# A fused attention, mixture-of-experts and gated-convolution kernel: routing steps, copies and weight splits moved, and one product done in halves of 64 columns

## The chip, the cores and the metric

One Trainium2 chip, one core of it. The metric is the device time of one launch in microseconds (us).

## The reference

Float32 throughout; B=2 batches, S=768 tokens, 8 heads of 64, so rows of D=512. Three stages follow each other.

```python
# 1. decaying linear attention, per batch and head
state = gamma * state + outer(k[t], v[t]);  y[t] = q[t] @ state / 8
# 2. mixture of 8 experts, one per token, with a sticky choice
logits = x @ w_gate;  local_gate = sigmoid(x @ w_local)
e = argmax(logits[s]) if s == 0 or local_gate[s] < 0.5 else prev_e
out[s] = softmax(logits[s])[e] * (relu(x[s] @ w1[e]) @ w2[e])    # 512 -> 1024 -> 512
# 3. gated convolution over tokens
h = relu(x @ w_in);  c = conv1d(h, conv_w, 3 taps)
out = (h * sigmoid(c)) @ w_out                                   # 512 -> 1024 -> 512
```

The weights of stage 3 arrive as float64 and are decoded on the chip.

## The kernel before

**Attention** runs over 12 tiles of 128 tokens (6 per batch), and each tile's steps are written out by hand. For tile i TensorE does Z (q times the state so far, `a_Z`), X of tile i-1 (`a_X`), AV (`a_AV`: masked scores A times v), U (`a_U`: the state's update) and S of tile i+1 (`a_S`: q times k). X multiplies a tile's transposed output xT by xw, a matrix of identity blocks with the gate's columns beside them: it turns the tile so that tokens are on partitions and gives the routing logits (128 columns and 9) at once. ScalarE copies xT, the state Z, the tile xo that goes to the scratch tensor scr in DRAM, builds the decay tables (`a_table`) and scales half of v; GpSimd scales the other half of v (`a_scale_v`) and q of the tile after the next (`a_scale_q`); VectorE masks the scores (L352) and does the routing. The constants are one array in DRAM: the table tq is loaded in two halves (L1106), the rest as one tile C (L1107) that also holds the factors gv (for v) and gq (for the tables). Ten small products at the start (`keep_warm`) keep TensorE busy until q is there.

**Routing** (`route`) handles the tiles in groups of 3, 3, 3, 2 and 1. It is a generator: `part(g)` runs one more step of group g (the largest logit and a code; a scan that finds the last fresh choice; the one-hot matrix; counts; slots). `logits(i)` copies a tile's logits out of PSUM (L440, L441).

**Experts.** Each weight unit (128 x 1024) is loaded into one of 4 raw buffers (`load_unit`, on SP's queue), cast by ScalarE to its high part whi (`split_first`, L172) and subtracted by VectorE to its low part wlo (`split_second`, L181); then its raw buffer is free for the next load. Every product of the experts is three: high x high, high x low, low x high. Expert 0 starts before routing has ended, as half an expert (`alone(0, 0)`) on 128 rows gathered early (x0); `back` turns a layer's result with four transposes, after which VectorE makes its low part hl (L644). Then comes a branch for overflowing experts (`overflow`, not taken here), then the other half (`alone(0, 1)`, fed by `T(0, (1,))`, which makes xsh and xsl, L585), then experts 1 to 6 whole (`L1`, `L2`), and expert 7 in two halves. Between these, `dec_first` and `dec_second` decode stage 3's weights: two operations of ScalarE, five of VectorE (L218 to L224) and two last ones (L226, L227) on GpSimd or, where `last=nc.vector` says so, on VectorE. Near the end of expert 7 the rows of stage 3 are gathered (`c_gather`), scaled by VectorE (`c_scale`, L938) and transposed (`c_T`, L946).

All engines run their instructions in the order in which this code issues them, which is the order of the work; a read of a PSUM bank by ScalarE waits for an earlier read of that bank by VectorE.

Of the kernel before, what the change touches and what calls it, by code (L numbers as in the profile page):

```python
# [97 lines left out]
def tile_kernel(ctx: ExitStack, tc: tile.TileContext, consts, qk, kv, w1, w2, w_in, conv_w, w_out, out):  # L98
# [28 lines left out]
    n0 = off["gv"][0]  # L127
# [3 lines left out]
    def cv(name):  # L131
        a, b = off[name]
        return C[:, a - n0:b - n0]
# [132 lines left out]
    tabs = [ld.tile([P, NP * P], F32, name="tq", tag="tq", bufs=1)]  # L266
# [52 lines left out]
    def a_scale_q(i, engine, a=slice(0, 2)):  # L319
# [5 lines left out]
        engine.tensor_tensor(out=t, in0=t, in1=tabs[i % NC].rearrange("p (a n) -> p a n", a=2)[:, a], op=ALU.mult)  # L325

    def a_scale_v(i):
        if i >= NT:
# [10 lines left out]
    def a_S(i, ms=(0, 1)):  # L339

        t = qk_t[i]
        for m in ms:
# [5 lines left out]
        if ms[-1] == 0:  # L348
            return
# [50 lines left out]
    def a_X(i):  # L400
# [3 lines left out]
        for p in range(NP):  # L404
            o = (p % 2) * P
            nc.tensor.matmul(x_t[i][p // 2][:, o:o + XN], lhsT=xT[:, p, :], rhs=xw[:, p, :],
                             start=(p % 2 == 0), stop=(p % 2 == 1), skip_group_check=True)

    def a_store(i):
# [9 lines left out]
        nc.scalar.dma_start(out=scr[1 + i * P:1 + (i + 1) * P, :], in_=xo)  # L419
# [23 lines left out]
    def route(g):  # L443
# [55 lines left out]
        else:  # L499
            ve.tensor_copy(c_, end)  # L500
        at_ = tmp([P, n, E], "at")
# [101 lines left out]
    def moe(mo):  # L603
        xg_t, xs_t, h_t = {}, {}, {}
# [24 lines left out]
        def alone(e, half, free):  # L629
# [5 lines left out]
            def back(f):  # L635
# [8 lines left out]
                nc.vector.tensor_tensor(out=hl[:, 4 * f:4 * f + 4, sl], in0=p3, in1=dst.bitcast(F32), op=ALU.subtract)  # L644
# [112 lines left out]
        next(first)  # L757
        part(g3)
        next(first)
        next(first)  # L760
        part(g4)
        part(g3)
        next(first)
        part(g4)
        part(g3)
        next(first)
        part(g4)
        split_second(nc.vector)
        next(first)
# [3 lines left out]
        gather(0, (1,))  # L773
        for _ in route_blocks():
# [45 lines left out]
        for n, _ in enumerate(alone(e, 1, True)):  # L820
            if 8 <= n < 12:
                c_scale(n - 8)
# [422 lines left out]
```

## Time and profile before

| what | value |
|---|---|
| time, three runs | 404.12, 404.28, 405.5 us; median 404.28 |
| the profiled execution | 404.91 us; its span 403.1 us |
| TensorE matmul (PE) busy | 390.5 us, 97% |
| VectorE (DVE) busy | 294.4 us, 73% |
| ScalarE (ACT) busy | 246.7 us, 61% |
| GpSimd (POOL) busy | 113.2 us, 28% |
| moved by DMA | 73.24 MB, 182 GB/s over the span |

The span is one execution as the profiler sees it, and the time of that execution holds a little besides. An engine's busy time is what it spends in instructions; records of matmuls overlap, so a wait shorter than a record's tail does not show as idle. The waits view lists idle time and the instruction that ended it. Attention lies at 0 to 62 us, expert 0 at 62 to 94, experts 1 to 6 to 233, expert 7 to 261, stage 3 to the end.

### The profile page before, as it was taken

What the parts mean: (1) busy time and instruction counts of PE and PEld (TensorE: products, weight loads), DVE (VectorE), ACT (ScalarE), POOL (GpSimd) and SP (SyncE); (2) the same over time, 40 slices, a digit from 0 to 9 for tenths busy, and PEclk for the clock granted to TensorE, in tenths of its full rate; (3) what the DMA queues carried; (4) which work ended last, traced back from release to release, by engine and by line L of the source; (5) the groups of instructions that cost most, each with busy time, mean ns of one, the idle gap of its engine ahead of it and who ended that gap; (6) DMA issues with size and microseconds to landing.
All of it is one profiled execution on the core that took longest, in us unless ns stands there. A gap on an engine that the chain in (4) does not pass through costs nothing.

```text
span 403.1 us, 7359 instructions
## 1 busy us (share of the span) xinstructions
PE 390.5 (97%) x2772; PEld 337.5 (84%) x2772; DVE 294.4 (73%) x548; ACT 246.7 (61%) x483; POOL 113.2 (28%) x106
## 2 busy tenths in 40 slices
PE   7999998889999999999999999899999999999996
PEld 3888885568989797988989777699979789998986
DVE  3369867976799999799998858769954626990350
ACT  4886653656867675676757563578845437971531
POOL 3555510365035244363634242441000000000000
PEclk9999999999999999999999999999999999999999
DMA  8999992688879888787978131532010010001002
GB/s 295 377 355 411 323 364 107 209 266 297 302 225 327 283 314 259 244 309 263 320 265 303 60 102 47 137 112 72 0 53 27 0 54 27 2 0 52 28 0 78
DMA packets 28087, 73.24 MB, mean 182 GB/s; under 512 B 3009, under 2 KB 3649, under 8 KB 28050
## 3 DMA queue, kind: packets, MB, share of 16 engines
q1 hardware_dynamic: 19506, 54.67, 38.8%
q10 hardware_dynamic: 6240, 10.55, 7.2%
q0 software_dynamic: 2304, 7.54, 6.1%
q8 instruction: 22, 0.36, 0.4%
q14 instruction: 15, 0.12, 0.1%
HBM read 62.26 MB, written 10.49 MB: 180 GB/s over the span
## 4 chain that ended last, share of the span: by engine, by line
PE 55%; DVE 11%; issue 5%; DMA 5%; ACT 2%; POOL 2%; DVEq 0%; ACTq 0%; POOLq 0%
PE c L1041 15%; PE b L989 12%; PE c L742 11%; PE rt L989 5%; DVE wlo L181 5%; PE b L710 4%; DMA raw<-in_moe_w_dram 3%; PE state L710 2%; PE rt L710 2%; DVE hl L717 1%; DMA yg<-scr,posi 1%; ACT whi L172 1%; PE b L652 1%; PE a L946 1%; DVE xsl L585 1%
## 5 line engine op out<-in xcount | busy, mean ns | idle before, releaser
L181 DVE TENSOR_TENSOR wlo<-raw,whi 128x1024 fp32r<-128x1024 f32 x64 | 87.4, 1388 | 11.8 <-ACT whi L172 11.3
L172 ACT CAST whi<-raw 128x1024 fp32r<-128x1024 f32 x64 | 66.8, 1056 | 40.9 <-PE c L742 20.4
L1008 DVE SCALAR_TENSOR_TENSOR cs<-hs,cw,cs 128x384 f32<-128x384 f32 x64 | 39.6, 619 | 30.1 <-ACT cs L1006 29.0
L226 POOL TENSOR_TENSOR dmf<-dmf,ds 128x512 f32<-128x512 f32 x12 | 24.9, 2075 | 83.7 <-DVE ds L224 52.4
L742 PE MATMUL c<-whi,hh 128*112 128x512 f32 x96 | 38.0, 395 | 0.0
L742 PE MATMUL c<-wlo,hh 128*112 128x512 f32 x96 | 37.5, 391 | 0.0
L989 PE MATMUL b<-x,whi 128*128 128x386 f32 x176 | 37.1, 340 | 0.2 <-ACT x L956 0.2
L1041 PE MATMUL c<-whi,gh 128*128 128x512 f32 x88 | 35.2, 399 | 0.0
L1041 PE MATMUL c<-whi,gl 128*128 128x512 f32 x88 | 34.9, 396 | 0.0
L1041 PE MATMUL c<-wlo,gh 128*128 128x512 f32 x88 | 34.7, 395 | 0.0
L989 PEld LDWEIGHTS b<-x,whi 128*128 128x128 f32 x176 | 31.2, 189 | 0.8 <-ACT x L956 0.6
L742 PE MATMUL c<-whi,hl 128*112 128x512 f32 x96 | 30.0, 394 | 0.5 <-DVE hl L717 0.5
L611 POOL DMA_INDIRECT xg<-scr,permi x15 | 20.0, 1336 | 26.6 <-DVE nbi L541 19.6
L710 PE MATMUL b<-xsl,whi 128*128 128x240 f32 x96 | 26.6, 277 | 0.4 <-DVE xsl L585 0.4
L710 PE MATMUL b<-xsh,whi 128*128 128x240 f32 x96 | 26.5, 276 | 0.0
L710 PE MATMUL b<-xsh,wlo 128*128 128x240 f32 x96 | 26.3, 274 | 0.0
L352 DVE TENSOR_TENSOR A<-b,mask 128x512 f32<-128x512 f32 x24 | 15.4, 685 | 11.3 <-PE b L346 11.3
L1012 ACT ACTIVATE sg<-cs 128x384 f32<-128x384 f32 x32 | 16.6, 519 | 9.4 <-DVE gl L1018 9.1
L742 PEld LDWEIGHTS c<-whi,hl 128*112 128x112 f32 x96 | 17.1, 181 | 6.3 <-DVE hl L717 2.2
L742 PEld LDWEIGHTS c<-whi,hh 128*112 128x112 f32 x96 | 17.4, 181 | 4.3
L227 POOL TENSOR_TENSOR wdec<-dmf 128x512 f32<-128x512 f32 x12 | 20.7, 1721 | 0.9
L742 PEld LDWEIGHTS c<-wlo,hh 128*112 128x112 f32 x96 | 17.4, 181 | 4.2
(254 smaller groups left out, 1013.2 us busy)
## 6 DMA issues: line engine op xcount, KB each, us to landing
raw<-in_moe_w_dram SPq DMA_DIRECT2D x64, 512.0 KB, 4.9
qk<-in_qk_dram SPq DMA_DIRECT2D x11, 512.0 KB, 6.2
kv<-in_kv_dram SPq DMA_DIRECT2D x11, 512.0 KB, 5.9
draw<-in_moe_w_in_dram SPq DMA_DIRECT2D x8, 512.0 KB, 5.3
draw<-in_moe_w_out_dram SPq DMA_DIRECT2D x8, 512.0 KB, 4.8
scr<-xo ACTq DMA_DIRECT2D x11, 256.0 KB, 6.3
out_dram<-os ACTq DMA_DIRECT2D x11, 256.0 KB, 2.0
scr<-ys ACTq DMA_DIRECT2D x10, 256.0 KB, 3.6
```

The lines of the kernel that those rows point to most:

```text
L172: nc.scalar.copy(hi, raw[u])
L181: engine.tensor_tensor(out=lo, in0=t, in1=hi.bitcast(F32), op=ALU.subtract)
L226: last.tensor_tensor(out=f, in0=f, in1=s.bitcast(F32), op=ALU.mult)
L227: last.tensor_tensor(out=out, in0=f, in1=a.bitcast(F32), op=ALU.add)
L352: nc.vector.tensor_tensor(out=A_t[i][j], in0=sc2[j].rearrange("p (a t) -> p a t", a=NP), in1=mask.unsqueeze(1).to_broadcast([P, NP, P]), o ...
L611: nc.gpsimd.indirect_dma_start(out=t, out_offset=None, in_=xrow, in_offset=bass.IndirectOffsetOnAxis(ap=permi[:, col:col + 1], axis=0))
L710: nc.tensor.matmul(o, lhsT=a[:, fs], rhs=b_[:, dt, OFF:], start=(dt == 0 and n == 0 and ft % 2 == 0), stop=(dt == KD - 1 and n == 2), skip ...
L742: nc.tensor.matmul(yp[t][0:P - o], lhsT=a[:, ft, t * P + o:(t + 1) * P], rhs=b_[:, ws], start=(ft == 0 and a is hh and b_ is wh), stop=(ft ...
L989: nc.tensor.matmul(pb[:, 0:WN], lhsT=split[u_in + dt][wi][:, fs], rhs=x_[dt // 2][:, dt % 2, :], start=(n == 0), stop=(n == 3 * KD - 1))
L1008: nc.vector.scalar_tensor_tensor(out=cs, in0=tap[j], scalar=cw[:, j, ft:ft + 1], in1=cs, op0=ALU.mult, op1=ALU.add)
L1012: nc.scalar.activation(out=sg, in_=cs, func=AF.Sigmoid)
L1041: nc.tensor.matmul(ops[t][:, 0:n_], lhsT=a[:, ts_], rhs=b_[:, ws], start=(ft == 0 and n == 0), stop=(ft == KF - 1 and n == 2))
```

## The change

Six edits, all in the order or the form of work; what is computed stays the same.

1. gv and gq move from C into the second half of tq's load. All of tile 0's v is scaled by GpSimd, in two instructions. `a_S0` does tile 0's scores in two PSUM bank pairs and masks them in halves. Nine warming products instead of ten.
2. X is done as eight products with 64 columns of xT each, the halves in turn on the two partition halves of the same bank.
3. In tile 10 one more weight unit is cast and split; in the last tile the split before `a_U` is done before `a_X`, and routing of the last group but one starts after `a_AV`. The store of tile 10 follows the copy of x_last.
4. Two weight loads go ahead of the two loads for the decode; routing steps between the first products of expert 0 are dealt out anew, with one more pause (`yield`) for small groups, and the first `hl` waits for two of them.
5. Splits, decodes and T around the branch: splits at steps 0 and 4, T before `dec_second`, the first decode wholly on VectorE; in the second half of expert 0 the decode starts three steps later.
6. `c_scale` one step earlier in expert 7.

```diff
-    n0 = off["gv"][0]
+    n0 = off["rev"][0]
...
-        return C[:, a - n0:b - n0]
+        return tabs[0][:, a:b] if b <= n0 else C[:, a - n0:b - n0]
...
-        nc.gpsimd.tensor_tensor(out=t[:, H // 2:], in0=t[:, H // 2:],
-                                in1=g[:, H // 2:].unsqueeze(2).to_broadcast([P, H // 2, D]), op=ALU.mult)
-        for h in range(H // 2):
+        for a in ((slice(0, H // 2), slice(H // 2, H)) if i == 0 else (slice(H // 2, H),)):
+            nc.gpsimd.tensor_tensor(out=t[:, a], in0=t[:, a], in1=g[:, a].unsqueeze(2).to_broadcast([P, H // 2, D]),
+                                    op=ALU.mult)
+        for h in range(H // 2 if i else 0):
...
+    def a_S0():
+
+        t = qk_t[0]
+        A_t[0] = [at.tile([P, NP, P], F32, name=f"A{j}", tag=f"A{j}", bufs=1) for j in range(2)]
+        for m in range(2):
+            a_scale_q(0, nc.vector, slice(m, m + 1))
+            for half in range(2):
+                for j in range(2):
+                    nc.tensor.matmul((sc2, x2)[m][j][:, half * P:(half + 1) * P], lhsT=t[HALF[j], m, 1, half, :],
+                                     rhs=t[HALF[j], m, 0, half, :], start=True, stop=True)
+        for m in range(2):
+            for j in range(2):
+                nc.vector.tensor_tensor(out=A_t[0][j][:, 2 * m:2 * m + 2],
+                                        in0=(sc2, x2)[m][j][:, 0:2 * P].rearrange("p (a t) -> p a t", a=2),
+                                        in1=mask.unsqueeze(1).to_broadcast([P, 2, P]), op=ALU.mult)
...
-            nc.tensor.matmul(x_t[i][p // 2][:, o:o + XN], lhsT=xT[:, p, :], rhs=xw[:, p, :],
-                             start=(p % 2 == 0), stop=(p % 2 == 1), skip_group_check=True)
+            for half in HALF:
+                nc.tensor.matmul(x_t[i][p // 2][half, o:o + XN], lhsT=xT[:, p, half], rhs=xw[:, p, :],
+                                 start=(p % 2 == 0), stop=(p % 2 == 1), skip_group_check=True)
...
+        if n < 3:
+            yield
...
+                if (e, half, f) == (0, 0, 0):
+                    low_first.append(low)
+                else:
+                    low()
...
-            if n in (0, 1, 2, 7):
+            if n in (0, 4):
                 split_unit(nc.vector)
             if n == 3:
                 overflow(mo)
                 gather(1)
-                dec_first()
-            elif n == 4:
-                dec_second()
+                dec_first(last=nc.vector)
             elif n == 5:
                 T(0, (1,))
+                dec_second()
         for n, _ in enumerate(alone(0, 1, True)):
             if n == 0:
-                dec_first()
-            elif n == 1:
+                split_unit(nc.vector)
+            elif n == 3:
+                dec_first(mo)
+            elif n == 5:
                 dec_second()
...
-            if 8 <= n < 12:
-                c_scale(n - 8)
+            if 7 <= n < 11:
+                c_scale(n - 7)
...
-        for half in range(2):
-            a_scale_q(0, nc.vector, slice(half, half + 1))
-            a_S(0, (half,))
+        a_S0()
...
             part(due)
+            if last_tile:
+                split_second(nc.vector, False)
             if i:
                 a_X(i - 1)
                 logits(i - 1)
-                a_store(i - 1)
-            if fresh is not None:
+                store = a_store(i - 1)
+                if not last_tile:
+                    store()
+            if i == NT - 2:
+                split_first()
+            if fresh is not None and not last_tile:
                 rts[fresh] = route(fresh)
                 part(fresh)
             a_AV(i)
+            if last_tile:
+                store()
+                rts[fresh] = route(fresh)
+                part(fresh)
...
+        load_unit()
+        load_unit()
         dec_load()
         dec_load()
-        load_unit()
```

VectorE in the last two tiles, before. A is the masked scores of tile 11, LG the logits of tile 10, x_last a copy that X of tile 11 reads, R and sl routing's counts and slots.

```order
L352 TENSOR_TENSOR A_987<-b_77,mask 128x512
L352 TENSOR_TENSOR A_988<-b_78,mask 128x512
L500 CAST cnt<-rt 128x8
...
L506 TENSOR_SCALAR sl<-slot_112,R_116 128x256 x3
L440 COPY LG<-c_79 128x9
L441 TENSOR_TENSOR LG<-c_80,LG 128x9
L458 TENSOR_REDUCE MX<-LG 128x2
...
L381 COPY x_last<-a_76 128x2x128
L181 TENSOR_TENSOR wlo<-raw,whi 128x1024
```

And now:

```order
L181 TENSOR_TENSOR wlo<-raw,whi 128x1024
L367 TENSOR_TENSOR A_1029<-b_77,mask 128x512
L367 TENSOR_TENSOR A_1030<-b_78,mask 128x512
...
L524 TENSOR_SCALAR sl<-slot_112,R_116 128x256 x3
L181 TENSOR_TENSOR wlo<-raw,whi 128x1024
L456 COPY LG<-c_79 128x9
L457 TENSOR_TENSOR LG<-c_80,LG 128x9
L396 COPY x_last<-a_76 128x2x128
L474 TENSOR_REDUCE MX<-LG 128x2
```

One split moved ahead of the logits' copy and one more was added ahead of the masks; the copy of x_last moved ahead of routing's step.

VectorE after the branch, in expert 0, before (ds and dmag belong to the decode, xsl is what the second half of expert 0 waits for, ys the first half's result):

```order
L218 TENSOR_SCALAR dmag<-dmag 128x512
L219 TENSOR_SCALAR dmag<-dmag 128x512
L221 TENSOR_SCALAR ds<-draw 128x512
L222 SCALAR_TENSOR_TENSOR dmag<-dmag,ds 128x512
L224 TENSOR_SCALAR ds<-dmag 128x512
L585 TENSOR_TENSOR xsl<-a_76,xsh 128x4x128
L181 TENSOR_TENSOR wlo<-raw,whi 128x1024
L687 COPY ys<-c_79 128x512
```

And now:

```order
L181 TENSOR_TENSOR wlo<-raw,whi 128x1024
L603 TENSOR_TENSOR xsl<-a_76,xsh 128x4x128
L218 TENSOR_SCALAR dmag<-dmag 128x512
...
L224 TENSOR_SCALAR ds<-dmag 128x512
L226 TENSOR_TENSOR df<-df,ds 128x512
L227 TENSOR_TENSOR wdec_86<-df,dmag 128x512
L713 COPY ys<-c_79 128x512
L181 TENSOR_TENSOR wlo<-raw,whi 128x1024
```

xsl moved ahead of the decode, behind one split, and the decode's last two operations came over from GpSimd.

SP's queue at the end of attention, before (raw are the weight units, draw the decode's loads) and now:

```order
L163 DMA raw<-in_moe_w_dram 128x2x512 x4
L244 DMA draw<-in_moe_w_in_dram 128x1024 x2
L161 DMA raw<-in_moe_w_dram 128x1024 x4
```

```order
L163 DMA raw<-in_moe_w_dram 128x2x512 x4
L161 DMA raw<-in_moe_w_dram 128x1024 x2
L244 DMA draw<-in_moe_w_in_dram 128x1024 x2
L161 DMA raw<-in_moe_w_dram 128x1024 x2
```

Two weight loads, the units 8 and 9, moved ahead of the two loads of the decode.

## Rows read from the trace of the kernel before

**Rows 1.** The windows view: share of time busy per engine, granted clock, DMA share, GB/s.

```profile
0.00:10.00 10.00, 7.35 (x59) 3.76 (x59) 3.69 (x9) 4.48 (x13) 3.73 (x17) 1.00 0.80 293
...
10.00:20.00 10.00, 10.00 (x171) 8.89 (x175) 3.42 (x9) 8.50 (x31) 5.14 (x9) 1.00 1.01 377
...
80.00:100.00 20.00, 17.86 (x104) 14.86 (x105) 15.18 (x18) 10.72 (x15) 12.83 (x9) 1.00 0.83 278
```

**Rows 2.** Timeline, first 10 us: start, length, engine, line, out<-in, count, wait before.

```profile
5.18 0.42 DVE L325 TENSOR_TENSOR qk<-qk,tq 128x256 f32<-128x256 f32 x1 [0.51 <-DMA tq<-in_consts_dram]
...
5.83 1.16 PE L346 MATMUL b<-qk 64*128 64x128 f32 x16
...
7.04 0.61 POOL L332 TENSOR_TENSOR kv<-kv,C 128x256 f32<-128x256 f32 x1 [5.06 <-DMA C<-in_consts_dram]
...
7.81 1.43 PE L374 MATMUL a<-A,kv 128*64 128x128 f32 x16 [0.82 <-ACT kv L335]
...
9.25 0.69 DVE L325 TENSOR_TENSOR qk<-qk,wdec 128x512 f32<-128x512 f32 x1 [0.94 <-ACT wdec L316]
...
9.99 1.16 PE L346 MATMUL b<-qk 64*128 64x128 f32 x16 [0.29 <-DVE qk L325]
```

**Rows 3.** Timeline of attention tile 2: TensorE, and what ScalarE and GpSimd do beside it.

```profile
15.89 1.06 ACT L335 ACTIVATE kv<-kv,C 128x64 f32<-128x64 f32 x4
...
16.00 1.21 PE L406 MATMUL c<-xw,xT 128*128 128x137 f32 x8
...
16.08 1.27 POOL L325 TENSOR_TENSOR qk<-qk,wdec 128x512 f32<-128x512 f32 x1 [1.13 <-DMA qk<-in_qk_dram]
...
17.14 1.09 PE L374 MATMUL a<-A,kv 128*64 128x128 f32 x16
...
18.06 0.63 PE L396 MATMUL state<-kv 128*64 128x64 f32 x16
```

**Rows 4.** Timeline, end of attention and expert 0's first half: VectorE, ScalarE, TensorE.

```profile
56.96 1.04 ACT L172 CAST whi<-raw 128x1024 fp32r<-128x1024 f32 x1
...
59.09 0.16 DVE L440 COPY LG<-c 128x9 f32<-128x9 f32 x1
...
60.41 0.37 ACT L383 COPY x_last<-a 128x256 f32<-128x256 f32 x1 [0.45 <-ACT xo L416]
...
61.12 1.22 DVE L181 TENSOR_TENSOR wlo<-raw,whi 128x1024 fp32r<-128x1024 f32 x1
...
71.48 0.39 PE L671 MATMUL c<-whi,hh 128*128 128x512 f32 x1
```

**Rows 5.** The waits view of TensorE, 62 to 160 us: total, times, longest.

```profile
PE a L640 <- ACT hr L663: 1.0, 1, 1.0
...
PE b L652 <- DVE xsl L585: 1.0, 1, 1.0
...
PE rt L484 <- DVE far L470: 0.6, 1, 0.6
```

**Rows 6.** Timeline around expert 0's second half and the entry of expert 1.

```profile
79.92 0.68 DVE L585 TENSOR_TENSOR xsl<-a,xsh 128x512 fp32r<-128x512 f32 x1
...
80.52 2.25 DVE L181 TENSOR_TENSOR wlo<-raw,whi 128x1024 fp32r<-128x1024 f32 x1
...
95.48 0.38 PE L710 MATMUL b<-xsl,whi 128*128 128x240 f32 x1 [0.40 <-DVE xsl L585]
```

**Rows 7.** The chain that ended last: two of its pieces (start, length, what).

```profile
96.59 8.42 DMA raw<-in_moe_w_dram
...
154.32 10.29 PE c L742 x44
```

**Rows 8.** The waits view of TensorE, 160 us to the end.

```profile
PE rt L946 <- DVE yg L938: 0.5, 1, 0.5
...
PE a L946 <- DVE yg L938: 0.4, 1, 0.4
```

**Rows 9.** Timeline at the end of expert 7.

```profile
253.93 0.48 DVE L938 TENSOR_SCALAR yg<-yg,G_all 128x512 f32<-128x512 f32 x1
```

More of the change, by code (lines that the diff above doesn't have):

```diff
@@ L265, in tile_kernel @@
     at = att.enter_context(tc.tile_pool(name="at", bufs=2))
-    tabs = [ld.tile([P, NP * P], F32, name="tq", tag="tq", bufs=1)]
+    tabs = [ld.tile([P, n0], F32, name="tq", tag="tq", bufs=1)]
     mask = ld.tile([P, P], F32, name="mask", tag="mask", bufs=1)
@@ L324, in a_scale_q @@
         t = qk_t[i][:, a, 0].rearrange("p a c t -> p a (c t)")
-        engine.tensor_tensor(out=t, in0=t, in1=tabs[i % NC].rearrange("p (a n) -> p a n", a=2)[:, a], op=ALU.mult)
+        engine.tensor_tensor(out=t, in0=t, in1=tabs[i % NC][:, 0:NP * P].rearrange("p (a n) -> p a n", a=2)[:, a], op=ALU.mult)
     def a_scale_v(i):
@@ L331, in a_scale_v, with a_S @@
         g = cv("gv")[:, c * H:(c + 1) * H]
-        nc.gpsimd.tensor_tensor(out=t[:, H // 2:], in0=t[:, H // 2:],
-                                in1=g[:, H // 2:].unsqueeze(2).to_broadcast([P, H // 2, D]), op=ALU.mult)
-        for h in range(H // 2):
+        for a in ((slice(0, H // 2), slice(H // 2, H)) if i == 0 else (slice(H // 2, H),)):
+            nc.gpsimd.tensor_tensor(out=t[:, a], in0=t[:, a], in1=g[:, a].unsqueeze(2).to_broadcast([P, H // 2, D]),
+                                    op=ALU.mult)
+        for h in range(H // 2 if i else 0):
             nc.scalar.activation(out=t[:, h], in_=t[:, h], func=AF.Copy, scale=g[:, h:h + 1])
     HALF = (slice(0, D), slice(D, P))
-    def a_S(i, ms=(0, 1)):
+    def a_S0():
[12 more added lines that the diff above has]
+                                        in1=mask.unsqueeze(1).to_broadcast([P, 2, P]), op=ALU.mult)
+    def a_S(i):
         t = qk_t[i]
-        for m in ms:
+        for m in range(2):
             for half in range(2):
@@ L347, in a_S @@
                                      start=True, stop=True)
-        if ms[-1] == 0:
-            return
         A_t[i] = [at.tile([P, NP, P], F32, name=f"A{j}", tag=f"A{j}", bufs=1) for j in range(2)]
@@ L418, in a_store @@
                                "p k (half d) -> p k half d", half=2))
-        nc.scalar.dma_start(out=scr[1 + i * P:1 + (i + 1) * P, :], in_=xo)
+        return lambda: nc.scalar.dma_start(out=scr[1 + i * P:1 + (i + 1) * P, :], in_=xo)
     def small(shape, name, dt=F32):
@@ L603, in moe @@
     def moe(mo):
-        xg_t, xs_t, h_t = {}, {}, {}
+        xg_t, xs_t, h_t, low_first = {}, {}, {}, []
         def gather(e, halves=(0, 1)):
@@ L643, in back, with low @@
                 nc.scalar.copy(dst, p3)
-                nc.vector.tensor_tensor(out=hl[:, 4 * f:4 * f + 4, sl], in0=p3, in1=dst.bitcast(F32), op=ALU.subtract)
+                def low():
+                    nc.vector.tensor_tensor(out=hl[:, 4 * f:4 * f + 4, sl], in0=p3, in1=dst.bitcast(F32),
+                                            op=ALU.subtract)
+                if (e, half, f) == (0, 0, 0):
+                    low_first.append(low)
+                else:
+                    low()
             for f in range(2):
@@ L757, in moe @@
         next(first)
+        next(first)
         part(g3)
@@ L761, in moe @@
         part(g4)
+        next(first)
         part(g3)
+        part(g4)
         next(first)
+        part(g3)
         part(g4)
+        part(g4)
+        low_first.pop()()
+        next(first)
         part(g3)
[L766 to L769, printed above, removed]
         next(first)
@@ L773, in moe @@
         gather(0, (1,))
+        split_second(nc.vector)
         for _ in route_blocks():
@@ L1104, in tile_kernel @@
         for half in range(2):
-            n = slice(half * n0 // 2, (half + 1) * n0 // 2)
+            n = slice(half * NP * P // 2, (NP * P // 2, n0)[half])
             nc.scalar.dma_start(out=tabs[0][:, n], in_=consts[:, n])
@@ L1113, in tile_kernel @@
         nc.vector.memset(x_last, 0.0)
-        keep_warm(10)
+        keep_warm(9)
         nc.vector.memset(small_zero, 0.0)
@@ L1192, in tile_kernel @@
         logits(NT - 1)
-        a_store(NT - 1)
+        a_store(NT - 1)()
         split_first()
```

## The prediction

> **What bounds the kernel now.** I read the windows first, then the chain of waits, TensorE's waits, and the timeline wherever TensorE idles. TensorE is busy 7.35 of the first 10 us, all of the next 10, and 17.86 of the 20 from 80 us on [rows 1]. The chain shows who is ahead of it: up to 154 us it runs through VectorE's weight splits and weight loads (one load alone is 8.42 us of it), and from 154.32 us TensorE follows itself, 44 products at a time [rows 7]. So time can come back in four places: the first tile, TensorE's own work in attention, the stretch from attention to expert 1, and the short waits at the end of expert 7 [rows 8]. What VectorE or ScalarE do beside a busy TensorE costs nothing. DMA is saturated in attention (share 1.01 [rows 1]), so an earlier TensorE also has to find its tiles loaded.
>
> The sum is made against the profiled execution, 404.91 us (span 403.1), which is 0.63 above the median of the three runs, 404.28; what it gives is taken off the median.
>
> **First tile.** Today AV of tile 0 starts at 7.81, after waiting 0.82 on ScalarE's scaling of v; GpSimd's half began only at 7.04, held by the table C [rows 2]. S of tile 1 starts at 9.99, held by VectorE's scaling of q at 9.25, which waited 0.94 for a table that ScalarE built only after scaling v [rows 2]. Now the factors gv and gq arrive with the second half of tq, which had landed by 5.18 [rows 2]; the half grows from 256 to 328 columns, some 0.1 us. GpSimd scales both halves of v (0.61 each [rows 2]), ScalarE builds the table at once, and A of tile 0 is masked in halves as the products come. When v and the second tile's q land is not shown: v between 5.18 and 7.04, q of tile 1 by 9.25. At best S of tile 1 follows AV and U without a pause from about 6.7, i.e. 1.4 earlier than 9.99; at worst q lands so late that 0.5 is left. From the bytes ahead of it (1.9 MB at some 0.37 MB/us once the queues run, from the 293 GB/s mean [rows 1]) I put q at 7.3 to 8.3, and take **-1.1** (-0.5 to -1.4). The tenth warming product ended about when S could start; one fewer costs nothing, since S takes its place. The limit behind it: q of tile 3 is scaled from 16.08, when its load lands, for 1.27 [rows 3], so S of tile 3, back to back with U (which starts at 18.06), can come at most some 1.2 us earlier.
>
> **The product with xw (X).** Four products 128 columns wide take 16.00 to 17.14, 1.14 us; AV, eight products 64 wide that pair on the two column halves, takes 17.14 to 18.06, 0.92, for 128 moving columns [rows 3]. Scaled to 137 columns a paired X takes 0.92 x 137/128 = 0.98, so 0.16 less per tile, 1.9 over 12 tiles. It counts only where TensorE is alone on the path. ScalarE's four scalings of v end at 16.95, 0.19 before AV begins [rows 3], and the tiles that carry routing hang on VectorE as well. So between 0.2 and 1.9; I take half: **-1.0**.
> The Trainium skill, page "TensorEngine Tiling (Array Packing)", sections "Theoretical Speedup" and "Instruction Overhead", speaks against this edit: it promises a gain only to products of at most 64 columns, which X is not, and charges each matmul about 60 cycles. Estimated by that page, four more matmuls a tile would add about 0.1 us at 2.4 GHz, 1.2 over 12 tiles, and the sum would be 404.28 - 1.1 + 1.2 - 0.5 - 0.6 = 403.3.
>
> **Attention to expert 1.** Three moves, on VectorE's queue.
> (a) One weight unit more is cast and split before the last tile's logits. Its cast (1.04 [rows 4]) goes ahead of the copy of tile 10's xT and makes the mask of tile 11 wait some 0.6; the next split (1.22) stands right before the copy of the logits, now at 59.09 [rows 4]. The copies out of the same bank, x_last (60.41) and X of tile 11 queue behind it: late by 1.3 to 1.9. A DMA issue goes too: the store of tile 10 now follows x_last.
> (b) Behind that, routing is interleaved so that what a product needs is asked for one product earlier. Today x_last's copy ends at 60.78 [rows 4], X takes 1.14 behind it, so expert 0's products begin near 62.0, and its second layer at 71.48 [rows 4]: 9.5 us for 24 products of 0.23 (10.29/44 [rows 7]), 5.6 us, and small routing products that I estimate at 1.5 to 2. Some 2 us are waits, 0.6 of them on the scan [rows 5]. With the new order I find none, so the late start is about paid back: 0, +-0.7.
> (c) After the branch the subtraction for xsl (0.68 at 79.92) no longer stands behind five operations of the decode but ahead of them, so the 1.0 that TensorE waits for it goes [rows 5, 6]. So does the other 1.0, on ScalarE's hr [rows 5], since the second decode starts after hr. Neither is free time at the end: VectorE is, by my count, then full from about 77 to the entry of expert 1, whose third product waits on xsl until 95.48 [rows 6]. What counts is VectorE's work ahead of that: one split fewer (-1.2); the first decode's last two operations come to it from GpSimd (+1.4, at the 0.68 of an operation of that size), but without GpSimd beside it a split takes 1.22 and not 2.25 (-1.0) [rows 4, 6]; the second decode now lies three steps later, so GpSimd's part falls on the last splits, 0 to +1.0.
> Sum of (a) to (c): -0.8 to +0.2; with the 0.7 of (b) -1.2 to +0.8, and I take **-0.5**. From there to 154 us each link of the chain follows the one before, so the shift is carried on.
> The loads: on SP units 8 and 9 go ahead of the two decode loads, which then wait for a free buffer until about 61; the first is needed only by the decode that ends at 79.92 [rows 6], so some 13 us cover it. That fills DMA time that idles today.
>
> **End of expert 7.** The scaling of the gathered rows begins at 253.93, behind hl [rows 9]; one step earlier it stands before hl, and the last of the four before a split. Waits of 0.4 and 0.5 on it [rows 8] can go. Now VectorE can stop at the gather's landing with hl behind it. Bounds 0 and -0.9; I take **-0.6**: the scaling waited for no load at 253.93 [rows 9], so the first gather lies before that, how far is not shown.
>
> Sum: -1.1 - 1.0 - 0.5 - 0.6 = -3.2, so 404.28 - 3.2 = **401.1 us** (the profiled execution would be 401.7). Fewer columns of C, cv's second table and the moved reading of novi cost nothing that TensorE waits for.
>
> **Rivals.**
> (A) The late start of (a) is not paid back: tile 11's X and the first expert product come 1.7 late, some routing wait stays, and VectorE enters expert 1 later by as much. For it: the split lies right in the path from X of tile 10 to x_last. Against it: the waits of [rows 5] stood behind this order. Then +1.2 (-0.5 and 1.7) instead of -0.5: 404.28 - 2.1 + 1.2 - 0.6 = 402.8, and 403.6 if X brings only 0.2.
> (B) X gains nothing, because each of the eight products pays for its own start and weights: it stays at 1.14, so 401.1 + 1.0 = 402.1. Against it: AV and U are eight products each and differ in the moving columns alone, 128 and 64; they run 1.09 and 0.63, and twice the difference, 0.92, is all that AV takes [rows 3], so no fixed part shows. That is the rule of the skill's page named above; the rows speak against it.
> (C) Slower: the two halves of X do not run at once, because both stream the same 137 columns and write one bank, which no product of today does in quite this way. Each half would take 1.14/4 = 0.285, eight of them 2.28, so +1.14 on each of 12 tiles, 13.7: 404.28 - 2.2 + 13.7 = 415.8. It decides from +0.35 per tile on. Against it: AV's halves share a bank too.
> (D) The change does not do what it says at the start, because v or q lands late: -0.5 for -1.1, so 401.7. This lies inside the forecast.
>
> **Chances.** Forecast with (D), 399.4 to 402.3: 0.62. (A) 0.24. (B) 0.08, of which half is below 402.3. (C) 0.03, and 0.03 for a new wait that I don't see. About 0.5%, 2 us, is what a measurement of this kernel tells from no change: below 402.3 faster, above 406.3 slower. Faster 0.66, same 0.28, slower 0.06. All bounds on the good side together give 398.9; the range takes all but 0.5 of them, and (A) on the other side: 399.4 to 403.8.
>
> **What would show it.** S of tile 1 near 8.9, not 9.99. X in 0.98 per tile. x_last's copy late by more than a microsecond against the tile before it, no wait on far or xsl afterwards, expert 1's third product 2.5 us or so before 95.48. No wait on yg. I'm wrong if X takes 1.14 or more, if TensorE waits for q in tiles 2 to 4, or if expert 1 begins where it begins today.

## The result, and the profile after

The changed kernel takes **410.04 us** (median of four runs, 408.83 to 411.51) against 404.25 for the kernel before on the same chip: 1.4% slower, ratio 1.0142 (95% interval 1.012 to 1.0163). The forecast was 401.1 and faster, with a range of 399.4 to 403.8. The profiled execution took 410.64 us, its span is 408.9.

Lines in the changed kernel lie 15 to 31 higher: L640 is now L658, L652 L678, L671 L697, L710 L736, L742 L768, L989 L1020; the relu hr is L689, xsl L603, ys's copy L713 and its store L715, the third stage's cast and subtraction L987 and L990.

TensorE's waits, 62 to 160 us, then 160 us to the end (who waits, for whom, total, times, longest), after:

```profile
PE b L736 <- DVE xsl L603: 2.6, 1, 2.6
PE a L658 <- ACT hr L689: 2.5, 1, 2.5
PE c L697 <- PEq L864: 0.7, 1, 0.7
PE a L658 <- DMA draw<-in_moe_w_in_dram: 0.6, 1, 0.6
...
PE b L1020 <- ACT x L987: 2.0, 1, 2.0
PE rt L977 <- DVE yg L969: 0.3, 1, 0.3
```

Against [rows 5]: the waits for far and for expert 0's xsl are gone, as forecast, and that for hr has grown from 1.0 to 2.5. The xsl wait at the entry of expert 1 grew from 0.40 [rows 6] to 2.6, and the start of the third stage, which waited 0.2 before, waits 2.0.

The windows view after (busy time of each engine, then the granted clock, DMA share, GB/s):

```profile
80.00:85.00 5.00, 2.91 (x13) 2.02 (x11) 3.38 (x7) 1.18 (x2) 0.33 (x1) 1.00 0.97 329
85.00:90.00 5.00, 4.58 (x18) 3.66 (x19) 3.83 (x6) 3.52 (x6) 0.00 (x0) 0.66 0.41 125
...
100.00:105.00 5.00, 5.00 (x33) 5.00 (x33) 2.82 (x3) 2.77 (x4) 1.58 (x2) 0.69 0.96 337
...
265.00:270.00 5.00, 4.47 (x19) 4.37 (x20) 1.70 (x9) 2.38 (x9) 0.00 (x0) 0.69 0.14 52
```

Behind each of the three long waits the granted clock falls to 0.66 to 0.69 over 5 us. The timeline shows how: from 85.83 to 88.81 products of 512 columns follow each other every 0.43 us instead of 0.23, the lower of TensorE's two levels, 1.2 instead of 2.4 GHz. [Rows 1] show 1.00 from 80 to 100 us.

Where the time went, read off the two timelines (start in us):

| instruction of TensorE | before | after | difference |
|---|---|---|---|
| S of tile 1 | 9.99 | 9.62 | -0.37 |
| S of tile 11 | 55.60 | 54.35 | -1.25 |
| X of tile 11 | 60.83 | 60.76 | -0.07 |
| expert 0, first half, second layer | 71.48 | 70.62 | -0.86 |
| second half, third product | 80.65 | 78.91 | -1.74 |
| its turn of hr (first wait) | 85.70 | 85.42 | -0.28 |
| its second layer | 87.60 | 88.38 | +0.78 |
| expert 1, third product (second wait) | 95.48 | 98.73 | +3.25 |
| expert 1, second layer | 106.98 | 111.84 | +4.86 |
| expert 7, second half, second layer | 251.11 | 254.53 | +3.42 |
| third stage (third wait) | 261.18 | 265.53 | +4.35 |
| end of the span | 403.1 | 408.9 | +5.8 |

At 78.91 the change is 1.74 us ahead. Against before, the three waits then cost 1.46, 2.2 and 0.93, and the low clock behind them 1.3, 1.6 and 1.45. These are shares of TensorE's own timeline; the 1.3 would not come back by itself, as the first experiment shows. Between experts 1 and 7 the kernel gets 1.4 back: it arrives later, and the waits that expert 1 to 4's second layers had before (11.14 to 11.66 us each) are gone (11.00 to 11.04).

The first wait in the timeline after (start, length, engine, line, operation, idle time before it and what ended it):

```profile
81.40 0.69 DVE L226 TENSOR_TENSOR df<-df,ds 128x512 f32<-128x512 f32 x1
82.12 0.69 DVE L227 TENSOR_TENSOR wdec<-df,dmag 128x512 f32<-128x512 f32 x1
82.73 0.68 DVE L713 COPY ys<-c 128x512 f32<-128x512 f32 x1
83.82 1.04 ACT L172 CAST whi<-raw 128x1024 fp32r<-128x1024 f32 x1 [6.17 <-DVE ys L713]
84.78 0.59 ACT L689 ACTIVATE hr<-b 128x512 f32<-128x512 f32 x1
84.90 1.23 DVE L181 TENSOR_TENSOR wlo<-raw,whi 128x1024 fp32r<-128x1024 f32 x1 [1.49 <-ACT whi L172]
...
85.42 0.66 PE L658 MATMUL a<-ident,hr 128*128 128x128 f32 x4 [2.51 <-ACT hr L689]
...
86.25 0.63 PE L678 MATMUL rt<-wlo,xsh 128*128 128x512 f32 x1
86.67 0.63 PE L678 MATMUL rt<-whi,xsl 128*128 128x512 f32 x1
...
87.02 0.69 DVE L664 TENSOR_TENSOR hl<-a,hh 128x512 fp32r<-128x512 f32 x1 [0.89 <-ACT hh L661]
...
87.96 1.23 DVE L181 TENSOR_TENSOR wlo<-raw,whi 128x1024 fp32r<-128x1024 f32 x1 [0.25 <-ACT whi L172]
```

The decode's operations stand on VectorE's queue ahead of the copy of ys, whose product had ended at 78.4. The store of ys is issued by ScalarE, waits for that copy, and holds ScalarE's own queue for 6.17 us: the next cast and hr stand behind it, and TensorE behind hr. VectorE waits for ScalarE too: it stands idle for 1.49, 0.89 and 0.25 us, 2.63 in all, on its way to expert 1's xsl.

The second wait, in the same view:

```profile
91.73 1.29 POOL L226 TENSOR_TENSOR dmf<-dmf,ds 128x512 f32<-128x512 f32 x1 [11.41 <-ACT whi L172]
92.02 4.32 DVE L181 TENSOR_TENSOR wlo<-raw,whi 128x1024 fp32r<-128x1024 f32 x2
...
93.10 2.16 POOL L227 TENSOR_TENSOR wdec<-dmf 128x512 f32<-128x512 f32 x1
...
98.73 0.38 PE L736 MATMUL b<-xsl,whi 128*128 128x240 f32 x1 [2.62 <-DVE xsl L603]
```

Two splits beside GpSimd take 4.32 us together. And the third:

```profile
259.34 0.49 DVE L969 TENSOR_SCALAR yg<-yg,G_all 128x512 f32<-128x512 f32 x1 [0.28 <-DMA yg<-scr,posi]
...
260.74 0.71 DVE L969 TENSOR_SCALAR yg<-yg,G_all 128x512 f32<-128x512 f32 x1 [0.91 <-DMA yg<-scr,posi]
...
261.37 0.73 DVE L990 TENSOR_TENSOR x<-a,x 128x256 fp32r<-128x256 f32 x2
...
261.86 0.70 ACT L987 CAST x<-b 128x256 fp32r<-128x256 f32 x2 [2.33 <-DVE x L990]
...
265.53 0.97 PE L1020 MATMUL b<-x,whi 128*128 128x386 f32 x4 [1.99 <-ACT x L987]
```

The fourth scaling waits on VectorE for the fourth fetch with the subtraction of the rows already turned behind it. That subtraction ends the wait of ScalarE's next cast (of the other bank, b), and so on to the third stage. Before, the subtraction (L959) came first, and the fourth scaling (L938) then waited for nothing:

```profile
256.61 0.74 DVE L959 TENSOR_TENSOR x<-a,x 128x256 fp32r<-128x256 f32 x2
...
258.40 0.48 DVE L938 TENSOR_SCALAR yg<-yg,G_all 128x512 f32<-128x512 f32 x1
```

### The profile page after: what moved, and what is told of

Its sections match the earlier page's. It is cut to its first block, busy times and chain, and to the rows that moved or that the text cites. A ratio compares the mean times of both kernels' runs of the same rounds, so it can differ in the third digit from the quotient of the medians.

```text
span 408.9 us, 7547 instructions
## 1 busy us (share of the span) xinstructions
PE 392.5 (96%) x2867; PEld 342.3 (84%) x2867; DVE 296.5 (73%) x552; ACT 246.3 (60%) x479; POOL 110.6 (27%) x105
## 4 chain that ended last, share of the span: by engine, by line
PE 72%; DVE 4%; ACT 2%; issue 2%; DMA 1%; POOL 0%; ACTq 0%; DVEq 0%
PE c L768 16%; PE c L1072 15%; PE b L1020 12%; PE b L736 8%; PE rt L1020 5%; PE state L736 4%; PE rt L736 4%; PE b L678 1%; PE a L600 1%; PE c L697 1%; DVE wlo L181 1%; PE a L977 1%; DMA yg<-scr,posi 1%; ACT whi L172 1%; PE b L1072 1%
## 5 line engine op out<-in xcount | busy, mean ns | idle before, releaser
L226 POOL TENSOR_TENSOR dmf<-dmf,ds 128x512 f32<-128x512 f32 x13 | 26.2, 2013 | 94.0 <-DVE ds L224 64.8
L1020 PE MATMUL b<-x,whi 128*128 128x386 f32 x176 | 38.3, 348 | 2.0 <-ACT x L987 2.0
L768 PE MATMUL c<-whi,hh 128*112 128x512 f32 x96 | 38.0, 396 | 0.0
L768 PE MATMUL c<-wlo,hh 128*112 128x512 f32 x96 | 37.5, 391 | 0.0
L1020 PEld LDWEIGHTS b<-x,whi 128*128 128x128 f32 x176 | 32.3, 195 | 2.6 <-ACT x L987 2.4
L768 PE MATMUL c<-whi,hl 128*112 128x512 f32 x96 | 29.6, 390 | 0.0
L736 PE MATMUL b<-xsl,whi 128*128 128x240 f32 x96 | 26.8, 279 | 2.6 <-DVE xsl L603 2.6
L736 PE MATMUL b<-xsh,whi 128*128 128x240 f32 x96 | 26.7, 279 | 0.0
L736 PE MATMUL b<-xsh,wlo 128*128 128x240 f32 x96 | 26.6, 277 | 0.0
L227 POOL TENSOR_TENSOR wdec<-dmf 128x512 f32<-128x512 f32 x13 | 22.8, 1755 | 1.0
L768 PEld LDWEIGHTS c<-whi,hl 128*112 128x112 f32 x96 | 17.4, 181 | 4.5
L768 PEld LDWEIGHTS c<-whi,hh 128*112 128x112 f32 x96 | 17.4, 181 | 4.3
L768 PEld LDWEIGHTS c<-wlo,hh 128*112 128x112 f32 x96 | 17.4, 181 | 4.2
L736 PEld LDWEIGHTS b<-xsl,whi 128*128 128x128 f32 x96 | 18.5, 193 | 2.8 <-DVE xsl L603 2.8
```

Of the source, the lines that this page charges most:

```text
L226: last.tensor_tensor(out=f, in0=f, in1=s.bitcast(F32), op=ALU.mult)
L227: last.tensor_tensor(out=out, in0=f, in1=a.bitcast(F32), op=ALU.add)
L736: nc.tensor.matmul(o, lhsT=a[:, fs], rhs=b_[:, dt, OFF:], start=(dt == 0 and n == 0 and ft % 2 == 0), stop=(dt == KD - 1 and n == 2), skip ...
L768: nc.tensor.matmul(yp[t][0:P - o], lhsT=a[:, ft, t * P + o:(t + 1) * P], rhs=b_[:, ws], start=(ft == 0 and a is hh and b_ is wh), stop=(ft ...
L1020: nc.tensor.matmul(pb[:, 0:WN], lhsT=split[u_in + dt][wi][:, fs], rhs=x_[dt // 2][:, dt % 2, :], start=(n == 0), stop=(n == 3 * KD - 1))
```

## The experiments

Theory: three new waits and the low clock behind them make the loss; the rest of the change gains. All times are medians. A ratio is against the kernel before as it ran beside the same kernels: 404.54 beside c_fill, c_ys, c_dec2 and c_three, 404.21 beside c_four, c_old2, b_x and b_front, 404.27 beside c_four7, b_ys, d_nox and d_noft, 404.31 beside c_gps, 404.10 beside c_nogp and c_dve2. Times of different groups are best compared by their ratios.

### The clock by itself: products for nothing in the waits

```diff
+ if (e, half) == (0, 1): fill(20)     # ahead of back(0)
+ if (e, dt, ft, n) == (1, 0, 0, 1): fill(22)     # in L1
+ if ft == 0: fill(16)     # ahead of h2(0, 0, 1)
```

> The changed kernel with matmuls whose result nobody reads put into its three long TensorE waits: 20 of 256 columns before the turn that waits for hr, 22 ahead of the first xsl product of expert 1, 16 ahead of the first product of the third stage. The chain of waits stays as it is. Theory (the clock falls because TensorE stood idle, and the products after each wait then run at half speed): the granted clock stays 1.00 in all three stretches after the waits and 1.3 + 1.6 + 1.5 = 4.4 us come back, 405.6 us. Rival (the clock falls for another cause, or the time is lost in the waits alone): 410 us, the low stretches stay.

c_fill: **407.82 us** (407.44 to 408.19), ratio 1.0074 (1.0051 to 1.0097). The clock is 1.00 in all three stretches:

```profile
85.00:90.00 5.00, 4.47 (x27) 3.26 (x25) 3.24 (x4) 4.25 (x8) 0.00 (x0) 1.00 0.55 199
...
100.00:105.00 5.00, 5.00 (x47) 5.00 (x46) 2.79 (x3) 1.62 (x2) 3.31 (x2) 1.00 0.86 312
...
265.00:270.00 5.00, 5.00 (x32) 4.97 (x31) 1.52 (x12) 2.83 (x7) 0.62 (x1) 1.00 0.14 52
```

So in these three places it is the idle engine that brings the clock down, and keeping it busy gives 2.2 us back: half of what I expected. Two reasons show. The first is that the first low stretch costs nothing at the end:

```profile
79.62 0.50 PE L682 MATMUL b<-whi,xsl 128*128 128x512 f32 x1 [0.24 <-DVE xsl L607]
...
99.44 0.38 PE L742 MATMUL b<-xsl,whi 128*128 128x240 f32 x1 [0.50 <-DVE xsl L607]
```

With the clock up, expert 1's third product still has to wait for xsl, and starts as much later than in the changed kernel (99.44 for 98.73, 0.71) as expert 0's second half already was ahead of any filling (its third product at 79.62 for 78.91). VectorE sets this point, and stands idle as before (1.49, 0.88 and 0.25 us). From there to the end the run takes 306.96 us against 310.17: the 1.6 and 1.45 of the other two stretches come back. The second reason is that the changed kernel doesn't lose the clock three times in each execution; the mean granted clock of single runs shows it:

```
after    410.64 0.987   411.51 0.988   409.44 0.992   408.83 0.996
c_fill   408.19 1.000   407.90 1.000   407.74 1.000   407.44 1.000
c_ys     407.33 0.992   407.90 0.992   407.96 0.992   408.49 0.992
         406.27 0.996   405.99 0.996   405.84 1.000
```

Steps of 0.004, about one us each.

### The first wait: ys's copy ahead of the decode

```diff
                 T(0, (1,))
-                dec_second()
+        dec_second()
         for n, _ in enumerate(alone(0, 1, True)):
```

> The changed kernel with the finish of the first decode moved from step 5 of the first half of expert 0 to behind that half, so behind the copy of ys on VectorE. Theory: the wait for hr (2.51 us) was ScalarE standing behind the store of ys, which waited for a copy queued behind the decode; it falls under 1 us and the clock does not fall at 85 us: up to 1.5 + 1.3 us at that place. Whether it reaches the end depends on the wait for xsl of expert 1: if that is set by TensorE's own pace, 407.2 us; rival (VectorE is the bound to the entry of expert 1, so what is saved waits there): 409 to 410 us.

c_ys: **407.33 us**, 2.7 less than the changed kernel, ratio 1.0067 (1.0043 to 1.0092). The wait for hr is gone, the clock stays at 1.00 from 80 to 100 us; the wait for xsl grows to 2.9. The theory's number holds, and the rival's reason with it: VectorE does set the entry of expert 1, but it now runs from 77.13 to the entry without a pause, and the third product starts at 95.81 instead of 98.73.

### The second wait: the second decode later

```diff
-            elif n == 5:
-                dec_second()
             if n == 9:
                 T(1, (0,))
             elif n == 11:
                 T(1, (1,))
+                dec_second()
                 gather(2)
```

> The changed kernel with the finish of the second decode moved behind the turning and splitting of expert 1's rows (step 5 to step 11 of the second half of expert 0). Theory: the two splits of 2.16 us beside GpSimd go back to 1.22 us and five VectorE steps of the decode leave the way of xsl, so the wait of 2.62 us falls under 0.5 us and the clock stays up: 2.2 + 1.6 us less, 406.2 us. Rival (the wait only moves into expert 1, behind the late decode): 409 to 410 us.

With all three places mended (this edit, the one before, and):

```diff
-            if 7 <= n < 11:
-                c_scale(n - 7)
+            if 8 <= n < 12:
+                c_scale(n - 8)
```

> Both moves together and the scalings of the gathered rows back at the steps they had before (8 to 11 instead of 7 to 10). Theory: all three waits and all three low stretches go, 5.8 us of loss and what attention gained is left over: 401 to 403.5 us, below the 404.25 of the kernel before. Rival (the rest of the reordering is worth nothing or costs): 404 us or above.

c_dec2 and c_three: **413.02** (ratio 1.0223, 1.0187 to 1.0258) and **407.36 us** (1.0061, 1.0041 to 1.0081): both theories fell, though the wait for xsl is down to 0.4. What the first one's rival said of the wait came true in both: it only moved. In the second of them TensorE now waits further on, and the clock falls to 0.63 from 105 to 110 us:

```profile
105.62 0.66 PE L600 MATMUL a<-ident,xg 128*128 128x128 f32 x4 [2.07 <-DMA xg<-scr,permi]
108.41 1.11 PE L600 MATMUL a<-ident,xg 128*128 128x128 f32 x4 [2.14 <-DMA xg<-scr,permi]
```

and on GpSimd the fetch that it waits for stands behind the decode's two steps, one line too low:

```profile
95.17 2.06 POOL L226 TENSOR_TENSOR dmf<-dmf,ds 128x512 f32<-128x512 f32 x1 [14.55 <-issue]
97.31 2.16 POOL L227 TENSOR_TENSOR wdec<-dmf 128x512 f32<-128x512 f32 x1
99.61 1.80 POOL L629 DMA_INDIRECT xg<-scr,permi  x1
```

GpSimd had been idle for 14.55 us. (The first of the two has the same waits for the fetch, 3.4 us together, beside the waits for hr and x that it keeps.) So I let the fetch go first:

```diff
                 T(1, (1,))
-                dec_second()
                 gather(2)
+                dec_second()
```

> As the run with all three places mended, but the fetch of expert 2's rows goes out ahead of the second decode and no longer behind its two GpSimd steps. Theory (in that run the 4.2 us wait for xg at the turn of expert 2's rows, and the low clock after it, came from the fetch standing behind the decode on GpSimd's queue): that wait falls under 1 us, no stretch is low, 402 to 403.5 us. Rival (the late decode holds up the loads that the fetch competes with): the wait stays over 1.5 us and the time at 405 us or more.

c_four: **402.25 us** (401.6 to 404.31) against 404.21, ratio **0.9958** (0.994 to 0.9976): faster than both kernels, with these as its longest waits from 62 to 160 us:

```profile
PE a L658 <- DMA scr<-xol: 1.0, 1, 1.0
PE c L697 <- PEq L863: 0.7, 1, 0.7
PE b L736 <- DVE xsl L603: 0.4, 1, 0.4
PE c L768 <- DVE hl L743: 0.3, 1, 0.3
```

and a mean clock of 1.0 in the profiled execution. The order of two lines on GpSimd's queue was worth 5 us. With the second decode at its old steps instead:

```diff
             if n == 0:
                 split_unit(nc.vector)
-            elif n == 3:
                 dec_first(mo)
-            elif n == 5:
+            elif n == 1:
                 dec_second()
```

> The changed kernel with the first decode's finish behind the copy of ys, the second decode back at the steps it had before (start at 0, finish at 1 of the second half of expert 0) and the scalings back at 8 to 11. Theory: the two GpSimd steps of that decode lie before the splits that xsl waits for, as before; the wait for xsl is under 1 us and the fetch of expert 2's rows is early: 402 to 403.5 us. Rival (VectorE has more to do than the time to expert 1 holds, wherever the decode stands): the wait for xsl stays over 1.5 us, 405 to 407 us.

c_old2: **404.93 us** (1.0011, 1.0001 to 1.0021). The wait for xsl is 0.8, as the theory had it, but the time is the rival's: VectorE's steps of the decode now stand ahead of hl, and TensorE waits 2.2 us for that.

### Which part of the second decode made the second wait

```diff
             elif n == 5:
-                dec_second()
+                for _ in range(2):
+                    next(dec_raw["g"])     # the five VectorE steps
...
                 T(1, (1,))
                 gather(2)
+                dec_second()     # the two GpSimd steps
```

> The changed kernel with ys's copy ahead of the first decode's finish and the scalings at 8 to 11; of the second decode only the two GpSimd steps move, behind the splits of expert 1's rows and the fetch of expert 2's; its five VectorE steps stay where the change put them. Theory (GpSimd beside the two splits made them 2.16 us each instead of 1.22): the wait for xsl at the entry of expert 1 falls from 2.9 us to about 1 us, 403 to 404 us. Rival (the five VectorE steps of the decode, 2.7 us ahead of xsl, made the wait): it stays over 2 us, 404.5 to 406 us.

c_gps: **405.31 us** (1.0025, 1.0009 to 1.004), wait 2.8. That says nothing on the question: the two steps, written later, ran at the same point, beside the two splits. The fetch that now stands ahead of them had gone out by 83.9, and then they waited only for VectorE, whose fifth step ends at 88.96:

```profile
82.97 0.95 POOL L629 DMA_INDIRECT xg<-scr,permi  x1 [0.31 <-issue]
89.10 1.28 POOL L226 TENSOR_TENSOR dmf<-dmf,ds 128x512 f32<-128x512 f32 x1 [5.18 <-ACT whi L172]
89.48 4.22 DVE L181 TENSOR_TENSOR wlo<-raw,whi 128x1024 fp32r<-128x1024 f32 x2
```

Against the run with ys's copy alone it is 2.0 us less (1.7 by the ratios), with the scalings at steps 8 to 11 and an earlier fetch of expert 2's rows, which this run does not tell apart. Then without GpSimd at that place:

```diff
-                dec_first(mo)
+                dec_first(mo, last=None)     # None: nc.scalar.copy(out, f) for both steps
```

> As the run before this one in its first two edits (copy of ys ahead of the first decode's finish, scalings at 8 to 11), the second decode where the change put it, but its two GpSimd steps are left out: a copy on ScalarE stands for them, so that one 128x512 piece of the third stage's first weights is not decoded. Theory (GpSimd beside the two splits made them 2.16 us each): the two splits take 2.3 to 2.5 us together instead of 4.2 to 4.3 and the wait for xsl at the entry of expert 1 falls from 2.8 to about 0.9 us. Rival (VectorE's five steps): the splits or the wait stay as they were.

```profile
89.55 2.35 DVE L181 TENSOR_TENSOR wlo<-raw,whi 128x1024 fp32r<-128x1024 f32 x2
...
94.28 0.38 PE L739 MATMUL b<-xsl,whi 128*128 128x240 f32 x1 [0.96 <-DVE xsl L606]
```

With one piece of weights not decoded, the two splits take 2.35 us and the wait is 0.96, as the theory had it; c_nogp: **402.87 us** (0.9969, 0.995 to 0.9988). And on VectorE:

```diff
-                dec_first(mo)
+                dec_first(mo, last=nc.vector)
```

> The same with nothing left out: the two last steps of the second decode on VectorE instead of GpSimd. Theory: the splits take 2.3 to 2.5 us together, VectorE has 1.4 us more, so the wait for xsl falls by 0.5 us only, to 2.3 us. Rival: 2.8 + 1.4 = 4.2 us.

c_dve2: **403.92 us** (0.9985, 0.9967 to 1.0004). The splits again take 2.35, as the theory had it. Its 2.3 us for xsl did not come, nor the rival's 4.2: no wait for xsl is left, and one of 2.06 us for hl takes its place at the turn of expert 1's rows, so VectorE's five steps and the two last ones are paid at another point of the same queue:

```profile
90.93 0.66 PE L600 MATMUL a<-ident,xg 128*128 128x128 f32 x4 [2.06 <-DVE hl L664]
```

### The third wait by itself

```diff
-            if 8 <= n < 12:
-                c_scale(n - 8)
+            if 7 <= n < 11:
+                c_scale(n - 7)
```

> The version that was faster than both, with the scalings of the gathered rows at the changed kernel's steps 7 to 10. Theory (the fourth scaling waits on VectorE for the fourth fetch, ahead of the subtractions that TensorE's last stage needs): the wait for x at the start of that stage is 2.0 us again instead of 0.2 and the stage starts 0.9 us later; where the clock falls behind it, up to 1.5 us more: 403.2 to 404.7 us. Rival (earlier scaling is the gain that was forecast, and the wait came from the losses ahead of it): 401.7 to 402.3 us.

c_four7: **404.78 us** against 404.27 (1.0012, 0.9994 to 1.003), where the same kernel with steps 8 to 11 had 0.9958: the step costs 0.5%, about 2.2 us, just above the theory's range. In its profile the wait for x is 1.98 and the clock stays at 1.00 behind it (it is low at 5 to 15 us instead); the mean clock of 7 of its 12 runs is 0.996 or 0.992, and where the other six lose it is not shown.

### One suspect alone in the kernel before

```diff
-                dec_first()
-            elif n == 4:
-                dec_second()
+                dec_first(last=nc.vector)
             elif n == 5:
                 T(0, (1,))
+                dec_second()
```

> The kernel before with one thing of the change: its first decode in expert 0 finishes after the turn of the second half's rows instead of ahead of it, all on VectorE. Theory (the copy of ys queues behind the decode, and ScalarE's store, split and hr behind that): the wait for hr grows from 1.0 to 2.5 us, the clock falls behind it in most executions: 405.5 to 407.5 us. Rival (in the kernel before nothing waits for that copy, the routing's new order is needed too): 404 us, the wait for hr stays near 1 us.

b_ys: **405.60 us** (1.0025, 1.0008 to 1.0042), wait for hr 2.9. In the profiled execution the clock stayed up and the entry of expert 1 came 0.5 late (95.96): the wait for hr grew by 1.9, but the wait of 1.0 for expert 0's xsl ahead of it is gone, so the turn of hr comes only 0.5 late (86.17). Over the runs, three at a mean clock of 0.999 or more took 403.99 to 404.89, the seven at 0.995 or 0.996 took 404.73 to 406.53 (mean 405.65), and one at 0.992 took 406.29. As far as three runs can tell, most of the price here comes with the clock.

### What the parts that gain are worth

X in halves alone, in the kernel before:

```diff
-            nc.tensor.matmul(x_t[i][p // 2][:, o:o + XN], lhsT=xT[:, p, :], rhs=xw[:, p, :],
-                             start=(p % 2 == 0), stop=(p % 2 == 1), skip_group_check=True)
+            for half in HALF:
+                nc.tensor.matmul(x_t[i][p // 2][half, o:o + XN], lhsT=xT[:, p, half], rhs=xw[:, p, :],
+                                 start=(p % 2 == 0), stop=(p % 2 == 1), skip_group_check=True)
```

> The kernel before with the turning product X in pairs of 64 columns and nothing else. Theory: X takes 0.99 us a tile instead of 1.14 and attention's chain of 12 tiles runs through TensorE, so 1.0 us less, 403.3 us. Rival (the entry of the experts waits for the last tile's x or for the splits, whatever the tiles take): 404.3 us, no change.

b_x: **404.47 us** (1.0011, 0.9999 to 1.0023). Nothing, though X takes 0.99 a tile in its trace: the rival. Next the change up to the end of attention, so the changed kernel with routing, decodes and splits of expert 0 and the scalings as before; only this line of that part still differs from the kernel before:

```diff
-            if n in (0, 1, 2, 7):
+            if n in (1, 2, 7):
                 split_unit(nc.vector)
```

> The change up to the end of attention alone (first tile, X in halves, last tiles and loads), with routing, decodes and splits of expert 0 and the scalings as before, one split fewer in expert 0 since it is made in attention. Theory (the loss is all behind attention): between 402.5 and 403.8 us. Rival (the late x of the last tile and the split moved up cost what attention gained): 404.3 us or more.

b_front: **403.69 us** (0.9985, 0.9977 to 0.9994), as the theory had it: the loss lies behind attention. And two parts taken out of the fastest version, X whole again (the edit above, backwards) and the first tile as before (its tables, v and warming products too, not shown):

```diff
-        a_S0()
+        for half in range(2):
+            a_scale_q(0, nc.vector, slice(half, half + 1))
+            a_S(0, (half,))
```

> The version that was faster than both, with the turning product whole again (128 columns). Theory (X in halves is worth something only where VectorE and the loads leave room behind attention, which this version has): 403.0 to 403.4 us. Rival (X in halves is worth nothing here either, the last tile's x and the loads of attention set its end): 402.2 us.

> The version that was faster than both, with the first tile as in the kernel before. Theory (the first tile is worth the 0.4 us by which its second product S came earlier in the trace): 402.6 us. Rival (worth nothing: the loads of the first tiles set the pace): 402.2 us; forecast of old: 403.3 us.

d_nox and d_noft: **403.25** (0.9973, 0.9958 to 0.9988) and **402.86 us** (0.9968, 0.9954 to 0.9982), against 0.9958 with both: 0.6 and 0.4 us by the ratios, with intervals that overlap, so these two sizes are no more than likely. The other 0.7 of the 1.7 us that this version gains by its ratio is not split up further.

## Why the prediction was wrong

**First tile, -1.1.** Mis-sized: 0.37 in the trace, some 0.4 by the last run.

```profile
7.00 1.18 POOL L333 TENSOR_TENSOR kv<-kv,tq 128x256 f32<-128x256 f32 x2 [5.03 <-DMA kv<-in_kv_dram]
...
8.88 0.69 DVE L325 TENSOR_TENSOR qk<-qk,wdec 128x512 f32<-128x512 f32 x1 [0.59 <-DMA qk<-in_qk_dram]
...
9.62 1.16 PE L363 MATMUL b<-qk 64*128 64x128 f32 x16 [0.27 <-DVE qk L325]
```

v lands at 7.0 and q of tile 1 at 8.88: the loads set the pace, below even the low bound of 0.5. I had put q at 7.3 to 8.3 from a mean rate. This was rival (D), with a little less left than its 0.5.

**X, -1.0.** The mechanism was right, the size not:

```profile
15.43 1.16 PE L422 MATMUL c<-xw,xT 128*64 128x137 f32 x16
16.42 1.04 PE L389 MATMUL a<-A,kv 128*64 128x128 f32 x16
```

0.99 instead of 1.14, so rivals (B) and (C) fall. With them falls, in this case, what the Trainium skill's page "TensorEngine Tiling (Array Packing)", section "Instruction Overhead", charges for each matmul, about 60 cycles: four more of them made X shorter, not longer. Alone it is worth nothing that can be measured, with the rest mended perhaps 0.6.

**(a) and (b).** Right in the mechanism. TensorE is 1.25 ahead at S of tile 11 and 0.07 at X:

```profile
60.76 1.16 PE L422 MATMUL c<-xw,x_last 128*64 128x137 f32 x16 [1.46 <-ACT x_last L398]
```

The wait for x_last, 0.39 before, is 1.46, and 1.2 us are lost, just under the forecast's 1.3 to 1.9. The new order of routing then pays back 0.8 by 70.62, within the forecast. Rival (A), the largest at 0.24, did not come.

**(c) is the step that failed**, in three places. "So does the other 1.0, on ScalarE's hr [rows 5], since the second decode starts after hr": I followed the decode's operations, not what was queued around them. The copy of ys stood behind the first decode on VectorE, and behind it ScalarE's store, cast and hr: 1.0 became 2.5 instead of 0. "VectorE is, by my count, then full from about 77 to the entry of expert 1": behind the same store it stood idle for 2.63 us, and expert 1's xsl, which it makes, came later by as much. "GpSimd's part falls on the last splits, 0 to +1.0": it fell on the two splits ahead of xsl and cost 1.9 to 2.0 (4.22 to 4.32 instead of 2.35), although [rows 6] had shown a single split at 2.25 beside GpSimd. Two of those are 2 us, outside the range I gave.

**End of expert 7, -0.6.** Wrong in sign. The risk was named (VectorE can stop at the gather's landing) and not priced: the fourth scaling waits 0.91 for it, and what is behind it is not hl but the subtraction that the third stage hangs on. With the clock it costs some 2.2.

**What no step and no rival had** is the clock. The lower level never shows in the profile of before, where no wait late in the program was longer than about 1.0. I priced every wait at its length; in the profile of after, 1.3 to 1.6 us of slow products follow each of the three, and behind the last two they add to the end. A new wait that I didn't see had a chance of 0.03, and slower 0.06: of the signs that I had named, X, the lateness of x_last and the waits for far and expert 0's xsl came out; S of tile 1, the waits for yg and expert 1's third product (3.25 late, not 2.5 early) did not.

Summed from the runs (medians, with 404.1 to 404.5 for the kernel before beside them): first wait mended 410.04 to 407.33, third (with the fetch) to 405.31, GpSimd away from the splits to 402.87 and, with nothing left out, 402.25. The gains forecast, 3.2 us, were really about 2.

## What to carry to other kernels

When work is moved, list on each queue what then stands behind it, stores included: a store waits for its data and holds the engine that issues it (6.17 us here), and every engine that waits for that one. Moving a line later on an idle queue moved nothing in time here, and one line ahead of a fetch instead of behind it cost 5 us. And where a change makes a long TensorE wait (2.0 to 2.9 us here), count in that the products behind it may run at half speed for a while, and ask whether they or another engine set the next point.

## What the runs showed of the hardware that I had not expected

- Behind TensorE waits of 2.0 to 2.9 us, late in the program, the granted clock fell in 9 of the 13 cases in the profiles of these runs (two waits for xg close together counted once), and not in the other four (2.9 for xsl with ys's copy moved, 2.9 for hr in the kernel before with its decode moved, 2.2 for hl, 2.0 for x). The same kernel loses it in one execution and not in the next. Products for nothing in the wait kept it up in all four runs of c_fill.
- A VectorE split of 1024 columns with both inputs in SBUF takes about 1.17 us (2.35 for two), and 2.11 to 2.16 beside GpSimd's decode steps. The Trainium skill, page "SBUF — State Buffer", section "Who interferes with whom", says that such an instruction contends with a GpSimd one that reads SBUF: the trace agrees.
- In one profile (c_four7, the fastest version with the scalings at steps 7 to 10) the clock was at 0.82 and 0.84 from 5 to 15 us, where v landed at 7.46 and TensorE waited 1.57 us, and attention ended 2 us later (X of tile 11 at 62.87): at this size a single profile can mislead, and the medians decide.
